# ScalarE's instructions in the written order from batch 2 on, and a wider spacing of the softmax steps

## The chip, the cores and the metric

The kernel runs on one core of one Trainium2 chip. The metric is device time in microseconds for one execution of the whole program. Times without another source are from a profiled execution of the kernel before, counted from the start of its span. TensorE, VectorE, ScalarE and GpSimd compute; SyncE issues the transfers here.

## The reference

There are two parts: an attention over 32 learned slots, and a two-layer network (with ELU between the layers) on its result.

```
a    = softmax(phi, over the 576 positions)          # 8 batches, 8 heads, 576 x 32
k_m  = a^T k ;  v_m = a^T v                          # 32 x 64 per head
attn = softmax(q k_m^T / 8, over the 32 slots)       # 576 x 32
x    = attn v_m                                      # put together: 4608 x 512
h    = x w_in                                        # 4608 x 2048
g    = where(h > 0, h, exp(min(h, 0)) - 1)
out  = g w_out                                       # 4608 x 512
```

All is float32.

## The kernel before, in words

**The work.** The kernel never forms x. For each batch it multiplies `v_m` into `w_in` (the function `vw`), so that `hidden` gets h from the softmax's probabilities (the tile `A`) and that product in one step. A float32 product is made of three matmuls on a high and a low part of each factor, each in the faster format F32R. So nearly every operand is split in two instructions: a cast to the high part on ScalarE (a name with `_high` or `_parts`) and, on VectorE, a subtraction that leaves the low part (`_low`).

**The units.** The output is worked through in units, each half a batch by one block of 128 of the 2,048 hidden channels: 32 units a batch, counted on through the batches by the number `it`. In a half batch, 256 of its 288 rows go through `project2` at once; the 32 that are left over ("rest") are kept in the tile `rest` and multiplied after every second batch by `rest_project`. One unit from batch 2 on is this chain: `hidden` (L711, TensorE, into one of two banks `psh`), `elu_relu` (L835, ScalarE), `elu_exp2` (L840, ScalarE), `elu_max2` (L847 for the 256 rows and L849 for the rest, VectorE). L847 and L849 are the last readers of the bank, so a `hidden` waits for those of two units before. Two units make a pair. For a pair follow four sums on GpSimd (L859 to L862), the casts and remainders of the pair itself (`direct_parts`, L885 and L887, tile `GP` or `gS`) and of the sums (`sum_parts`, L893 and L894, tile `gS`), and on TensorE `project2` (L912), some three units after the pair's `hidden`. In batches 3 to 7, six of eight pairs of a half batch are multiplied in seven products instead of eight, which is what the sums are for.

**The attention of the next batch** is done between the units of the one before: `phi_max` (L441), `phi_exp` (L446), `e_shift` (GpSimd, L323), `e_exp` (ScalarE, L328), `slots` (L487), then for each of three parts of the batch `scores` (L536, into two banks `psb`), `turn` (VectorE, L559, which frees them), the softmax's steps `softmax_max`, `_shift`, `_exp` (ScalarE, L578), `_sum` (L584), `_divide`, `turn_back` (L601), and `probs_high` (ScalarE, L618) and `probs_low` (L626), which write `A`. Four times a batch comes `vw` (L536 too, also into `psb`) with `vw_high` (L656) and `vw_low` (L662). In batch 2, `w_out` is also combined for the seven products: `build_full` and `build_sums` on GpSimd (L789 to L798), `build_high` (L804), `build_low` (L811), and `save_t`, a store that SyncE issues.

**The rest products.** After every second batch come eight times `rest_high` (L1038), `rest_low` (L1043) and `rest_project` (L998), into two turns each of the tiles `GP` and `gS`, then `rest_store` (L1059) and its store. Two `hidden` of the next batch stand among the products on TensorE.

**What sets the order.** Up to the start of batch 2 the order of all engines is a long list, `FIRST`, written out by hand. From there `plan` is a list of steps, each with a place, a number in units:

```
def at(place, f, *a):
    if (f, a) not in done:
        plan.append((place, len(plan), f, a))
...
at(x, hidden, it)
at(x + 0.00001, elu_relu, it)
...
at(it - 0.4 + part, project2, it, part)
```

The plan is sorted by place. TensorE's instructions and SyncE's transfers stand exactly in that order. For ScalarE, VectorE and GpSimd the framework's scheduler chooses the order before the program runs: it takes the earliest step in the plan of those that its own reckoning says could start. At run time each engine takes its instructions in the order that was chosen, and an instruction that waits holds up those behind it.

Of the kernel before, what the change touches and what calls it, by code (L numbers as in the profile page):

```python
# [175 lines left out]
def fused_kernel(ctx: ExitStack, tc: tile.TileContext, phiT, phi, kv0, kvt, kv, q0, q1, w_in, w_out, out):  # L176
# [929 lines left out]
# [4 lines that stand above are left out]
    def softmax(b, u, o, step):  # L1110
        at(o, turn, b, u)
        at(o + step, softmax_max, b, u)
        at(o + 1.01 * step, softmax_shift, b, u)
        at(o + 2 * step, softmax_exp, b, u)
        at(o + 3 * step, softmax_sum, b, u)
        at(o + 3.01 * step, softmax_divide, b, u)
        at(o + 4 * step, turn_back, b, u)
        at(o + 5 * step, probs_high, b, u)
        at(o + 6 * step, probs_low, b, u)
# [6 lines left out]
    def attention(b, o):  # L1126

        x = 1 if b > NB else 0
        at(o - 4, load_phi, b)
        for c in range(NCH):  # L1130
            at(o - 3 + 5.5 * x + (1 - 0.2 * x) * c, load_kv, b, c)
        for u in range(3):
            at(o + 4 + 7.5 * x + u - 0.3 * x * u, load_q, b, u)
            at(o - 3 + u, load_e, b, u)
            at(o + 1.1 + 5.4 * x + u, e_shift, b, u)
            at(o + 2.1 + 5.4 * x + u, e_exp, b, u)
        at(o + 0.1 - 2 * x, phi_max, b)
        for g in range(2):
            at(o + 0.12 - 2 * x, phi_exp, b, g)
        at(o + 1.1, slot_scale, b)  # L1140
        at(o + 1 - 2.4 * x, spread_max, b)
        if b > NB:
            at(o + 2.2, fetch_max, b)
        for c in range(NCH):
            at(o + 5.4 + 5.8 * x, slots, b, c)
        at(o + 6.1 + 5.8 * x, slots_copy, b)
        at(o + 7.2 + 5.8 * x, slots_transpose, b)
        at(o + 7.4 + 5.8 * x, kv_copy, b)
        for u in range(3):
            i = o + 8.2 + 6.7 * x + (2 - 0.2 * x) * u  # L1150
            at(i, scores, b, u)
            softmax(b, u, i + 0.7, 0.3)

    LEAD = 30
    for b in range(2, B):
        base = 2 * NJ * b
        attention(b, 43 if b == 2 else base - LEAD)
        for c in range(NVC):
            for h in range(2 if b > NB else 0):
                at(base - 17 + 4 * c + h, load_w, b, c, h)  # L1160
            products(b, c, base - 10 + 4 * c if b > NB or c < 3 else base - 1.4)
# [58 lines left out]
                at(it + 4.6, rest_out, b // 2)  # L1220

    plan.sort(key=lambda x: x[:2])
    with tc.manual_schedule(engines={mybir.EngineType.PE, mybir.EngineType.SP}):
        with tc.manual_schedule():
            for f, a in first:
                f(*a)
        for _, _, f, a in plan:
            f(*a)
# [43 lines left out]
```

## Time and profile before

| | us |
|---|---|
| median of 3 runs | 769.75 (766.83 to 769.96) |
| the profiled execution | 768.35 |
| its span | 766.6 |
| TensorE busy (matmuls) | 711.2 |
| VectorE busy | 537.3 |
| ScalarE busy | 474.5 |
| GpSimd busy | 205.3 |

The span runs from the first to the last instruction; 1.75 us of the profiled execution lie outside it. Batch 2 begins at about 219 us. A row of a timeline gives start, duration, engine, line, operation, output tile and inputs, shapes and count; in brackets is the time for which the engine had been idle, and what ended it. A row with x12 stands for 12 instructions. A row of a table by stretches gives, after the length, the busy time (and count) of TensorE, its weight loads, VectorE, ScalarE and GpSimd, then the granted clock of TensorE, the share of the DMA engines and GB/s. A row of waits gives who waited for whom, the total in us, how often, and the longest.

### The profile page before, as it was taken

The page shows a single profiled execution, that of the slowest core. Times are in us where ns is not written, and L with a number is a line of the kernel's source. Part 1 is how long each engine was busy: PE and PEld are TensorE (multiplying, and loading weights), DVE is VectorE, ACT ScalarE, POOL GpSimd, SP SyncE. Part 2 cuts the span into 40 slices and gives each one's busy share as a digit, 9 for nine tenths or more (in the row PEclk, how much of TensorE's full clock was granted, in tenths as well). Part 3 has the DMA queues.
Part 4 walks back from the last instruction along what each step waited for, and adds up shares of the span by engine and source line. Part 5 has one row for each costly group of instructions (what it writes and reads, how often), then busy time and mean ns, then how long its engine had stood idle before and what let it go on. Part 6 is the DMA issues. An engine that isn't in the chain of part 4 may idle for free.

```text
span 766.6 us, 15955 instructions
## 1 busy us (share of the span) xinstructions
PE 711.2 (93%) x5974; PEld 604.8 (79%) x5974; DVE 537.3 (70%) x1329; ACT 474.5 (62%) x1146; POOL 205.3 (27%) x364
## 2 busy tenths in 40 slices
PE   7698999999987998999999999989999999999997
PEld 5566787878656876889788887888788988789996
DVE  3999898885674578556875568765786457875653
ACT  3779888886454556665565655665556555566661
POOL 0011111122036631242231432333231242323330
PEclk8799999999998999999999999999999999999999
DMA  9942526153354274786673976678848488464641
GB/s 296 350 175 80 195 81 241 63 204 90 117 127 144 90 275 166 234 310 259 249 278 114 305 276 251 267 233 292 312 173 286 127 298 315 181 242 172 220 165 41
DMA packets 44476, 158.97 MB, mean 207 GB/s; under 512 B 5232, under 2 KB 13552, under 8 KB 35952
## 3 DMA queue, kind: packets, MB, share of 16 engines
q1 hardware_dynamic: 44400, 157.97, 58.4%
q8 instruction: 47, 0.77, 0.4%
q14 instruction: 29, 0.24, 0.1%
HBM read 138.02 MB, written 19.93 MB: 206 GB/s over the span
## 4 chain that ended last, share of the span: by engine, by line
PE 54%; DVE 19%; POOL 9%; ACT 8%; DMA 5%; issue 4%; SPq 1%; DVEq 0%; ACTq 0%; POOLq 0%
PE psh L711 18%; PE pso L912 18%; PE pso L998 13%; DVE G L847 3%; PE psb L536 2%; POOL GF L861 2%; ACT gS L893 2%; PE psb L487 2%; POOL e L323 2%; POOL GF L859 2%; POOL GF L862 2%; DMA raw<-w_out 2%; DVE vw L662 1%; DMA kvt<-kvt 1%; DVE mx L566 1%
## 5 line engine op out<-in xcount | busy, mean ns | idle before, releaser
L711 PE MATMUL psh<-A,vw 128*128 128x288 f32 x1536 | 258.2, 305 | 24.4 <-DVE rest L849 18.5
L711 PEld LDWEIGHTS psh<-A,vw 128*128 128x128 f32 x1536 | 224.2, 191 | 60.7 <-issue 15.8
L912 PE MATMUL pso<-wout,gS 128*128 128x512 f32 (+1 forms) x612 | 145.5, 367 | 0.0
L998 PE MATMUL pso<-wout,GP 128*128 128x512 f32 x504 | 133.6, 400 | 3.2 <-DVE GP L757 2.3
L912 PEld LDWEIGHTS pso<-wout,gS 128*128 128x128 f32 x612 | 104.4, 191 | 14.6 <-ACT GP L885 0.8
L847 DVE SCALAR_TENSOR_TENSOR G<-G,psh 128x256 f32<-128x256 f32 x192 | 79.8, 416 | 48.6 <-ACT G L840 43.9
L998 PEld LDWEIGHTS pso<-wout,GP 128*128 128x128 f32 x504 | 90.1, 188 | 28.3 <-DVE GP L757 3.4
L835 ACT ACTIVATE G<-psh 128x288 f32<-128x288 f32 x192 | 77.6, 405 | 45.2 <-PE psh L711 42.8
L860 POOL TENSOR_TENSOR GF<-G 128x128 f32<-128x128 f32 x60 | 28.7, 479 | 231.3 <-DVE G L847 231.3
L840 ACT ACTIVATE G<-G 128x288 f32<-128x288 f32 x192 | 85.2, 444 | 4.8
L894 DVE TENSOR_TENSOR gS<-GF,gS 128x512 fp32r<-128x512 f32 x60 | 41.6, 693 | 51.8 <-ACT gS L893 51.5
L912 PE MATMUL pso<-tt,gS 128*128 128x256 f32 x540 | 75.8, 282 | 0.0
L893 ACT CAST gS<-GF 128x512 fp32r<-128x512 f32 x60 | 37.2, 621 | 61.4 <-POOL GF L862 59.4
L741 POOL COPY rest<-GF 128x32 f32<-128x32 f32 x64 | 24.4, 382 | 170.8 <-DVE GF L735 170.8
L912 PEld LDWEIGHTS pso<-tt,gS 128*128 128x128 f32 x540 | 69.9, 189 | 0.0
L887 DVE TENSOR_TENSOR GP<-G,GP 128x256 fp32r<-128x256 f32 (+1 forms) x120 | 55.8, 503 | 15.2 <-ACT GP L885 15.2
L912 PE MATMUL pso<-wout,GP 128*128 128x256 f32 x360 | 56.1, 288 | 0.0
L885 ACT CAST GP<-G 128x256 fp32r<-128x256 f32 (+1 forms) x120 | 36.8, 349 | 25.5 <-DVE G L847 20.8
L912 PEld LDWEIGHTS pso<-wout,GP 128*128 128x128 f32 x360 | 50.4, 196 | 0.0
L859 POOL TENSOR_TENSOR GF<-G 128x128 f32<-128x128 f32 x60 | 28.8, 479 | 67.2 <-DVE G L847 54.1
L662 DVE TENSOR_TENSOR vw<-psb,vw 128x512 fp32r<-128x512 f32 (+2 forms) x74 | 42.0, 602 | 2.4 <-ACT vw L656 2.2
L887 DVE TENSOR_TENSOR gS<-G,gS 128x512 fp32r<-128x512 f32 x36 | 26.5, 735 | 21.3 <-ACT gS L885 21.3
(135 smaller groups left out, 999.3 us busy)
## 6 DMA issues: line engine op xcount, KB each, us to landing
tt<-td SPq DMA_DIRECT2D x60, 1024.0 KB, 4.9
wt<-wd SPq DMA_DIRECT2D x40, 512.0 KB, 6.5
kvt<-kv SPq DMA_DIRECT2D x32, 512.0 KB, 8.5
out<-osb SPq DMA_DIRECT2D x16, 512.0 KB, 5.0
raw<-w_in SPq DMA_DIRECT2D x15, 512.0 KB, 7.3
raw<-w_out SPq DMA_DIRECT2D x15, 512.0 KB, 8.0
qt<-q SPq DMA_DIRECT2D x18, 384.0 KB, 5.2
td<-tt SPq DMA_DIRECT2D x6, 1024.0 KB, 4.9
```

Of the source, the lines that this page charges most:

```text
L662: nc.vector.tensor_tensor(t[:, LO, a, n0:n1], ps, t[:, HI, a, n0:n1], ALU.subtract)
L711: nc.tensor.matmul(ps, t[:, x, g, c0 : c0 + P], s["A"][hf][:, y, g, :], start=(n == 0), stop=(n == 5),)
L835: nc.scalar.activation(G[:, it % 2], gs[it], AF.Relu, scale=-1.0)
L840: nc.scalar.activation(G, G, AF.Exp, scale=-1.0)
L847: nc.vector.scalar_tensor_tensor(G[:, :n], G[:, :n], -1.0, ps[:, :n], ALU.add, ALU.max)
L859: eng.tensor_tensor(S[:, 0], a21, a22, ALU.add)
L885: nc.scalar.copy(f(HI), src)
L887: nc.vector.tensor_tensor(f(LO), src, f(HI), ALU.subtract)
L893: nc.scalar.copy(g[:, HI], S)
L894: nc.vector.tensor_tensor(g[:, LO], S, g[:, HI], ALU.subtract)
L912: nc.tensor.matmul(banks[bank_name][:, c0:c1], lhs(y), rhs(x), start=bank_name not in seen_banks, stop=stop and n == 2, skip_group_check=True,
L998: nc.tensor.matmul(ps, gp[:, y], wout[j][:, x, :], start=(first and n == 0), stop=(last and n == 2),)
```

## The change

```
-            softmax(b, u, i + 0.7, 0.3)
+            softmax(b, u, i + 0.7, 0.4)
...
-    with tc.manual_schedule(engines={mybir.EngineType.PE, mybir.EngineType.SP}):
+    with tc.manual_schedule(engines={mybir.EngineType.PE, mybir.EngineType.SP, mybir.EngineType.Activation}):
```

The first line moves the places of the softmax's steps: from `turn` on, they stand 0.4 instead of 0.3 of a unit apart, so `softmax_exp` stands 0.8 after `turn`, `probs_high` 2.0. `turn` itself stays. The second line takes ScalarE's order from the plan, word for word, as TensorE's and SyncE's are. VectorE and GpSimd are still ordered by the scheduler, which now reckons with another ScalarE. TensorE's order is the same instruction for instruction, and no instruction is added or taken away.

On ScalarE at the start of batch 2, from the second unit's Relu on. L1059 is `rest_store`, L804 `build_high`, L885 the first two pairs' `direct_parts`. Before:

```order
L1059 COPY orest<-pso_2511 128x512
L835 ACTIVATE G<-psh 128x288
L840 ACTIVATE G<-G 128x288
L656 CAST vw<-psb 128x512 x3
L804 CAST tt<-FE 128x512
L656 CAST vw<-psb 128x512
L885 CAST gS<-G 128x512
L835 ACTIVATE G<-psh 128x288
L804 CAST tt<-FE 128x512
L840 ACTIVATE G<-G 128x288
```

Now:

```order
L835 ACTIVATE G<-psh 128x288
L840 ACTIVATE G<-G 128x288
L656 CAST vw<-psb 128x512 x4
L835 ACTIVATE G<-psh 128x288
L840 ACTIVATE G<-G 128x288
L835 ACTIVATE G<-psh 128x288
L840 ACTIVATE G<-G 128x288
L1059 COPY orest<-pso_2511 128x512
L885 CAST gS<-G 128x512
```

The four `vw` casts and the next two units' Relu and Exp come first; `build_high` has gone back behind the twelfth unit, and the three `e_exp`, which stood behind the fifth unit, to places between the thirteenth and the sixteenth.

On ScalarE at the end of a softmax (that for batch 4 here; it is alike for batches 5 to 7). L656 is `vw_high`, L618 the last `probs_high`. Before:

```order
L893 CAST gS<-GF 128x512
L835 ACTIVATE G<-psh 128x288
L656 CAST vw<-psb 128x512
L840 ACTIVATE G<-G 128x288
L835 ACTIVATE G<-psh 128x288
L840 ACTIVATE G<-G 128x288
L618 CAST A<-pr 128x2x192
L885 CAST GP<-G 128x256
```

Now:

```order
L893 CAST gS<-GF 128x512
L835 ACTIVATE G<-psh 128x288
L840 ACTIVATE G<-G 128x288
L656 CAST vw<-psb 128x512 x2
L618 CAST A<-pr 128x2x192
L835 ACTIVATE G<-psh 128x288
L840 ACTIVATE G<-G 128x288
```

Relu and Exp of the first unit are no longer parted by a `vw_high`; `probs_high` has moved ahead of Relu and Exp of the second.

On ScalarE at the rest products after batch 3 (after batch 5 it is alike). L1038 is `rest_high`, L1059 `rest_store`; the L885 and L893 are the first pair's of the new batch. Before:

```order
L1038 CAST GP<-rest 128x256
L1038 CAST gS<-rest 128x256
L885 CAST GP<-G 128x256
L893 CAST gS<-GF 128x512
L835 ACTIVATE G<-psh 128x288
L840 ACTIVATE G<-G 128x288
L835 ACTIVATE G<-psh 128x288
L840 ACTIVATE G<-G 128x288
```

These are the seventh and the eighth `rest_high`. Now:

```order
L835 ACTIVATE G<-psh 128x288
L840 ACTIVATE G<-G 128x288
L835 ACTIVATE G<-psh 128x288
L840 ACTIVATE G<-G 128x288
L1038 CAST GP<-rest 128x256
L1038 CAST gS<-rest 128x256
L1059 COPY orest<-pso_4774 128x512
L885 CAST GP<-G 128x256
L885 CAST GP<-G 128x128
L446 ACTIVATE ph,sums<-ph,nm 128x576 x2
L893 CAST gS<-GF 128x512
```

The seventh and eighth `rest_high` now stand behind the two units whose `hidden` stand among the rest products on TensorE, and the first pair's casts behind `rest_store` and, for L893, behind both `phi_exp` (L446).

## The prediction

> **What bounds the kernel now.** I read, in this order, busy time by stage, who waited for whom, and the timelines round each stall of TensorE. First the stages from batch 2 on, summed (190 to 767 us).
>
> ```profile
> sum 577.00, PE 538.06 PEld 466.19 DVE 381.36 ACT 329.83 POOL 177.76; mean PE 89.68 PEld 77.70 DVE 63.56 ACT 54.97 POOL 29.63
> ```
>
> TensorE (second column) is busy for 538.06 of the last 577 us, ScalarE (fifth) for 329.83. So the time is TensorE's work in its fixed order plus its stalls, here 39 us; a new order on ScalarE can change only these, and what it makes other engines late for. Who ends them:
>
> ```profile
> PE psh L711 <- DVE rest L849: 18.5, 17, 5.1
> PE psb L536 <- DVE sc L559: 12.1, 7, 2.6
> ```
>
> `hidden` (L711) waits for VectorE to free one of two `psh` banks, and `scores` or `vw` (L536) for `turn`. VectorE does both only when ScalarE has done Relu and Exp in time. Eighteen microseconds and twelve are all that could be won there. A stall costs a second time:
>
> ```profile
> 374.00:377.40 3.40, 3.29 (x26) 2.67 (x27) 3.19 (x9) 2.21 (x6) 0.00 (x0) 0.58 0.73 290
> ...
> 296.00:299.40 3.40, 3.40 (x12) 2.94 (x12) 3.33 (x10) 3.17 (x8) 0.00 (x0) 0.51 0.46 189
> ...
> 649.00:652.40 3.40, 1.56 (x23) 0.95 (x22) 3.33 (x10) 1.45 (x4) 0.00 (x0) 1.00 1.05 430
> ```
>
> The third figure from the end is the granted clock. After stalls of 1.83 us (at 374) and 2.63 us (at 294) it was about half for 3.4 us, which is 1.7 us of work lost; after one of 1.84 us (at 651) it stayed at 1.00. I price a new stall of 1.8 to 2 us at half of 1.7, and one above 2.5 us at 1.7.
>
> **The change part by part.** No instruction is added or removed; TensorE's, and the loads', orders stay. All costs are shifts. Steady pairs keep ScalarE's order and cost nothing.
>
> *Start of batch 2.*
>
> ```profile
> 226.44 1.86 PE L711 MATMUL psh<-A,vw 128*128 128x288 f32 x12
> 233.43 1.78 PE L711 MATMUL psh<-A,vw 128*128 128x288 f32 x6 [5.12 <-DVE rest L849]
> ...
> 243.36 1.04 PE L711 MATMUL psh<-A,vw 128*128 128x288 f32 x6 [1.03 <-DVE rest L849]
> ...
> 225.98 0.59 ACT L656 CAST vw<-psb 128x512 fp32r<-128x512 f32 x1 [1.42 <-PE psb L536]
> 228.24 0.62 ACT L804 CAST tt<-FE 128x512 fp32r<-128x512 f32 x1 [1.67 <-POOL FE L797]
> 228.76 0.58 ACT L656 CAST vw<-psb 128x512 fp32r<-128x512 f32 x1
> 229.24 0.62 ACT L885 CAST gS<-G 128x512 fp32r<-128x512 f32 x1
> 229.76 0.41 ACT L835 ACTIVATE G<-psh 128x288 f32<-128x288 f32 x1
> ...
> 239.84 0.63 ACT L328 ACTIVATE e<-e 128x512 f32<-128x512 f32 x1 [3.70 <-POOL e L323]
> ...
> 323.69 0.88 PE L912 MATMUL pso<-tt,gS 128*128 128x256 f32 x6
> ```
>
> Before, `build_high` (L804) waits 1.67 us for GpSimd ahead of a Relu whose product was done at 227.4. Now the four `vw` casts end at 227.0, two Relu and Exp (0.85 us a pair) at 228.35 and 229.2, VectorE's two instructions after the first at 228.95, and `hidden` starts at 229.1, not 233.43. The row at 243.36 then falls near 237, since the wait at 239.84 and the half clock go as well: **-6.4**. `build_high` now waits some 10 units later; what covers it is that what it builds (`tt`) is first used in batch 3, at 323.69. If that cover failed, a store of about 5 us would stand in SyncE's queue before the loads of batch 3.
>
> *Softmax done during batch 2.*
>
> ```profile
> 286.51 0.79 PE L536 MATMUL psb<-qt,kvm 64*32 64x192 f32 x16 [1.29 <-DVE sc L559]
> ...
> 294.53 1.33 PE L536 MATMUL psb<-wt,kvm 64*32 64x256 f32 x32 [2.63 <-DVE sc L559]
> ...
> 289.61 1.22 DVE L811 TENSOR_TENSOR tt<-FE,tt 128x512 fp32r<-128x512 f32 x1
> ```
>
> `build_low` (L811) leaves its place ahead of the second and third `turn`. Followed through VectorE's new order with the durations of these rows, they come 1.0 and 3.0 us earlier, and the half clock after 294.53 goes: -4.7. At its end `probs_high` then holds up a Relu, as in the next part: a stall of 1.9 us and 0.85 of clock. Together **-2.0**.
>
> *The four later softmaxes* (batches 4 to 7).
>
> ```profile
> 374.11 1.00 PE L536 MATMUL psb<-qt,kvm 64*32 64x192 f32 x16 [1.83 <-DVE sc L559]
> ...
> 387.19 1.04 PE L711 MATMUL psh<-A,vw 128*128 128x288 f32 x6 [0.87 <-DVE rest L849]
> ...
> 389.14 0.96 PE L711 MATMUL psh<-A,vw 128*128 128x288 f32 x6
> ...
> 385.58 0.41 ACT L835 ACTIVATE G<-psh 128x288 f32<-128x288 f32 x1
> 386.02 0.44 ACT L840 ACTIVATE G<-G 128x288 f32<-128x288 f32 x1
> 387.59 0.52 ACT L618 CAST A<-pr 128x384 fp32r<-128x384 f32 x1 [1.12 <-DVE pr L601]
> ...
> 385.38 0.69 DVE L662 TENSOR_TENSOR vw<-psb,vw 128x512 fp32r<-128x512 f32 x1
> 386.98 0.58 DVE L601 STREAM_TRANSPOSE pr<-sc 128x384 f32<-128x384 f32 x1
> ```
>
> Three shifts. The first Exp of the scores now stands behind a pair's casts, its row sum follows on VectorE, and the second `turn` ends 0.7 us later: the stall of 1.83 becomes 2.5. Next the Exp ahead of the row at 387.19 no longer waits behind a `vw` cast, so that stall of 0.87 goes. Last, `probs_high` (L618) stands ahead of the Relu at 385.58. It waits for L601, which VectorE now does behind both `vw_low` (L662, 0.69 each): it ends about 388.85. So that Relu starts at 389.3, VectorE's L847 at 390.2 and L849 ends at 390.75; the `hidden` of 389.14 starts at 390.8 and the next one is 2.2 us late. From there TensorE runs with everything 2.2 us later. With half of 1.7 for the clock, 3.05 each: **+12.2**.
>
> *The rest products* (after batches 3 and 5).
>
> ```profile
> 413.46 1.77 PE L711 MATMUL psh<-A,vw 128*128 128x288 f32 x12
> 415.07 1.56 PE L998 MATMUL pso<-wout,GP 128*128 128x512 f32 x6
> ...
> 418.66 0.88 PE L912 MATMUL pso<-tt,gS 128*128 128x256 f32 x6
> ...
> 406.11 0.78 ACT L446 ACTIVATE ph<-ph,nm 128x576 f32<-128x576 f32 x1 [1.12 <-DVE nm L441]
> ...
> 410.87 0.41 ACT L1038 CAST gS<-rest 128x256 fp32r<-128x256 f32 x1 [0.99 <-PE pso L998]
> ...
> 413.71 0.62 ACT L893 CAST gS<-GF 128x512 fp32r<-128x512 f32 x1 [1.03 <-PE pso L998]
> ...
> 415.71 0.44 ACT L840 ACTIVATE G<-G 128x288 f32<-128x288 f32 x1
> ...
> 418.07 0.59 ACT L1059 COPY orest<-pso 128x512 f32<-128x512 f32 x1 [0.82 <-PE pso L998]
> ```
>
> Before, all eight `rest_high` (L1038) and the first pair's casts end by 414.3. Now the seventh and eighth `rest_high` stand behind Relu and Exp of the two `hidden` at 413.46, so behind 415.71: the seventh ends at 416.45, its remainder on VectorE, behind two L847 and L849, at 417.1, where TensorE wanted the first at 415.07. That is 1.85 us. Then L1059 waits for the last rest product (1.6 us after its start at 418.3), and the first pair's L885 (0.55), both `phi_exp` (0.77 each from start to start) and only then L893 follow: 419.9 + 0.5 + 0.55 + 1.54 = 422.5, ended at 423.1, its remainder at 423.85. The product of 418.66 cannot pass its first matmul before that: 5.1 us late, of which 3.2 is one stall, so 1.7 for the clock. Two such places: **+13.6**. Queued behind the waiting L893 are the second pair's casts and the next Relu; they keep up again within two pairs.
>
> *Single casts.*
>
> ```profile
> 513.52 1.04 PE L711 MATMUL psh<-A,vw 128*128 128x288 f32 x6 [0.80 <-DVE rest L849]
> ...
> 693.69 1.04 PE L711 MATMUL psh<-A,vw 128*128 128x288 f32 x6 [0.64 <-DVE rest L849]
> ```
>
> At both a Relu stood behind two `vw` casts; now it is ahead, and the stalls of 0.80 and 0.64 go; `phi_exp` and `e_exp` trade places with about nothing between them: **-1.4**.
>
> The sum: -6.4 - 2.0 + 12.2 + 13.6 - 1.4 = +16.0 us. Made against the profiled execution's 768.35 us (span 766.6 and 1.75 outside), it gives 784.4; the median of the runs, 769.75, is 1.4 above that execution. I predict **784 us**.
>
> The Trainium skill, in "TensorE: Matmul & The Clock Gate", section HAM oscillation, asks only that TensorE not idle for more than about 3.4 us. By that, no new stall here would cost clock. The row at 374 disagrees: 1.83 us sufficed. By the rule the sum is the first rival's below; by the row it stays.
>
> **Rivals.**
>
> *The clock holds.* As at 651, none of the new stalls halves the clock. Then 3.4 at the rests, 3.4 at the four softmaxes and 0.85 in batch 2 go: 776.7. For it: that one row. Against it: two stalls of 1.83 and 2.63 that did, and the new ones reach 3.2.
>
> *The softmax comes out even.*
>
> ```profile
> 374.00:381.00 7.00, 6.89 (x65) 6.07 (x73) 6.58 (x19) 3.94 (x10) 0.46 (x1) 0.76 0.36 143
> ```
>
> VectorE (fourth) works 6.58 of 7 us there, so a Relu that waits for L618 may only move work that VectorE would have done late anyway. Without the 12.2: 772.2, near no change. Against it: L847 behind a late Relu is what frees `psh`, and there are two banks.
>
> *Faster, by stock.*
>
> ```profile
> 389.77 0.62 ACT L893 CAST gS<-GF 128x512 fp32r<-128x512 f32 x1 [0.85 <-POOL GF L862]
> ...
> 393.40 0.87 PE L912 MATMUL pso<-wout,GP 128*128 128x256 f32 x6
> ```
>
> If TensorE had converted pairs in hand at the six places, it would run on while ScalarE waits, as between a pair's last cast at 389.77 and the pair's first product at 393.40. Then both positive terms go, the four 0.87 stalls go too, and batch 2's softmax wins its whole 4.7: 768.35 - 6.4 - 4.7 - 3.5 - 1.4 = 752.3. It decides from 3 us of stock. Against it: the products at 415.07 and 418.66 need exactly the casts that are moved, and none is in hand.
>
> *Backlog.* Each late place leaves ScalarE one pair behind; GpSimd's sums then come late for another pair, about 2 us more at six places: 796.
>
> **How the numbers follow.** Forecast 0.60, with its own spread of 778 to 790; clock 0.12; even 0.10; faster 0.07; backlog 0.11. A range of 772 to 794 leaves out the faster case, most of the backlog and a little of the rest. Half a percent, 3.8 us, is about what a measurement tells from no change: faster by more 0.08, within 0.11, slower by more 0.81.
>
> **What would show it.** Right: no stall above 1.5 us between 226 and 245, L811 after 245; TensorE waiting for L1038 or L1043 and then for L893 or L894 after batches 3 and 5; ScalarE waiting for L601 ahead of a Relu once a batch; more half-clock stretches after 300 us. Wrong: `rest_project` starting on time, or the `hidden` after the last `probs_high` within 0.5 us of its bank's turn; then the positive terms fall and the time is below 772.

## The result, and the profile after

The change makes the kernel slower: 790.94 us (median of 4 runs, 789.95 to 796.46) against 768.35 (4 runs, 766.83 to 769.96), a ratio of 1.031 with a 95% interval of 1.025 to 1.036. The forecast was 784 with a range of 772 to 794. The profiled execution took 790.94 us with a span of 789.2 (before: 768.35 and 766.6), at a mean granted clock of 0.970 (before 0.976).

The work is the same, so the 22.6 us between the two spans are waits and clock. From 190 us to the end, in the columns that the prediction's first row has:

```profile
sum 599.30, PE 543.15 PEld 471.04 DVE 387.24 ACT 332.66 POOL 177.83; mean PE 543.15 PEld 471.04 DVE 387.24 ACT 332.66 POOL 177.83
```

TensorE is busy 5.1 us longer than before (543.15 against 538.06), which is lower clock (nine windows of 3.41 us at half clock where there were six, 1.7 us each), and idle for 56 us where it had been idle for 39. Who ends its waits (microseconds in total, times, longest):

```profile
PE psh L711 <- DVE rest L849: 17.3, 12, 2.2
PE psb L536 <- DVE sc L559: 15.8, 8, 3.0
PE pso L912 <- ACT gS L893: 4.8, 2, 2.4
PE psh L711 <- ACT G L835: 4.5, 4, 1.1
...
PE pso L998 <- ACT GP L1038: 2.5, 2, 1.3
...
PE pso L912 <- DMA tt<-td: 2.0, 1, 2.0
```

The first two rows stood in the profile before with 18.5 and 12.1. The other four are new: a rest product waits for a cast (L1038), a pair's products for the cast of their sums (L893), `hidden` for a Relu (L835), and once, for 2.0 us, for a load (before, one such wait took 0.4). The timeline of TensorE shows where they stand; in brackets is the wait ahead of each row.

```profile
228.59 1.03 PE L711 MATMUL psh<-A,vw 128*128 128x288 f32 x6 [0.83 <-DVE rest L849]
...
325.34 0.62 PE L912 MATMUL pso<-tt,GP 128*128 128x256 f32 x3 [1.97 <-DMA tt<-td]
...
347.52 1.03 PE L711 MATMUL psh<-A,vw 128*128 128x288 f32 x6 [1.13 <-ACT G L835]
...
371.69 0.79 PE L536 MATMUL psb<-qt,kvm 64*32 64x192 f32 x16 [2.99 <-DVE sc L559]
...
387.52 1.78 PE L711 MATMUL psh<-A,vw 128*128 128x288 f32 x6 [2.23 <-DVE rest L849]
...
416.15 2.03 PE L998 MATMUL pso<-wout,GP 128*128 128x512 f32 x6 [1.27 <-ACT GP L1038]
...
422.79 0.38 PE L912 MATMUL pso<-tt,gS 128*128 128x256 f32 x1 [2.41 <-ACT gS L893]
```

TensorE's order is the same in both kernels, so any of its instructions can be found in both timelines, and how far it has moved says what lay before it. The table compares such instructions at the borders of the places that the prediction speaks of.

| place | the instruction at its end, before and after | moved there | the term measured | predicted |
|---|---|---|---|---|
| up to 226 us | L711, 226.44 and 225.91 | -0.5 | -0.5 | 0 |
| start of batch 2 | L912, 246.45 and 240.21 | -6.2 | -5.7 | -6.4 |
| softmax in batch 2 | L711, 319.65 and 312.78 | -6.9 | -0.6 | -2.0 |
| start of batch 3 | L912, 345.03 and 340.68 | -4.4 | **+2.5** | 0 |
| `e_exp`, four batches | first L487, 353.19 and 349.56 | -3.6 | **+3.8** (0.7, 1.0, 1.0, 1.0) | 0 |
| four later softmaxes | first L711, 396.87 and 396.61 | -0.3 | +13.4 (3.4, 3.7, 2.8, 3.5) | +12.2 |
| two rest products | first L912, 432.20 and 437.02 | +4.8 | +12.9 (5.1, 7.8) | +13.6 |
| single casts, three places | last L711, 700.06 and 722.49 | +22.4 | -3.1 | -1.4 |

For terms with several places the row names the end of the first (of the last for the single casts). Before rounding they make 22.6. What moved outside these places cancels: +0.8 at a wait of 1.00 us at 508.37 before, which has grown to 1.81 behind two `phi_exp`, and -1.1 between 603 and 622, with small steps elsewhere. The five that the prediction priced come to +16.9 where it had +16.0. What it lacks are the two rows in bold.

### The profile page after: what moved, and what is told of

It is laid out like the page before. It is cut to its first block, busy times and chain, and to the rows that moved or that the text cites. A ratio compares the mean times of both kernels' runs of the same rounds, so it can differ in the third digit from the quotient of the medians.

```text
span 789.2 us, 15976 instructions
## 1 busy us (share of the span) xinstructions
PE 715.6 (91%) x5974; PEld 608.9 (77%) x5974; DVE 543.1 (69%) x1329; ACT 477.7 (61%) x1146; POOL 205.3 (26%) x364
## 4 chain that ended last, share of the span: by engine, by line
PE 48%; DVE 19%; ACT 14%; POOL 8%; DMA 6%; issue 5%; SPq 0%; DVEq 0%; POOLq 0%; ACTq 0%
PE pso L912 16%; PE psh L711 15%; PE pso L998 12%; ACT G L840 3%; DVE G L847 3%; PE psb L536 3%; ACT G L835 3%; ACT gS L893 3%; POOL GF L861 3%; POOL GF L859 2%; POOL GF L862 2%; PE psb L487 2%; DVE vw L662 1%; DMA raw<-w_out 1%; DMA win<-w_in 1%
## 5 line engine op out<-in xcount | busy, mean ns | idle before, releaser
L711 PE MATMUL psh<-A,vw 128*128 128x288 f32 x1536 | 259.3, 305 | 26.8 <-DVE rest L849 17.3
L711 PEld LDWEIGHTS psh<-A,vw 128*128 128x128 f32 x1536 | 225.7, 192 | 60.7 <-ACT G L835 15.8
L912 PE MATMUL pso<-wout,gS 128*128 128x512 f32 (+1 forms) x612 | 144.3, 364 | 1.4 <-DVE gS L887 1.3
L998 PE MATMUL pso<-wout,GP 128*128 128x512 f32 x504 | 134.6, 401 | 6.1 <-ACT GP L1038 2.5
L847 DVE SCALAR_TENSOR_TENSOR G<-G,psh 128x256 f32<-128x256 f32 x192 | 80.4, 419 | 76.6 <-ACT G L840 70.9
L912 PEld LDWEIGHTS pso<-wout,gS 128*128 128x128 f32 x612 | 103.7, 190 | 16.1 <-DVE gS L887 1.6
L998 PEld LDWEIGHTS pso<-wout,GP 128*128 128x128 f32 x504 | 90.0, 188 | 32.8 <-ACT GP L1038 3.9
L835 ACT ACTIVATE G<-psh 128x288 f32<-128x288 f32 x192 | 77.6, 404 | 56.1 <-PE psh L711 55.2
L860 POOL TENSOR_TENSOR GF<-G 128x128 f32<-128x128 f32 x60 | 27.6, 460 | 235.2 <-DVE G L847 228.2
L912 PE MATMUL pso<-tt,gS 128*128 128x256 f32 x540 | 80.9, 294 | 5.3 <-ACT gS L893 4.8
L894 DVE TENSOR_TENSOR gS<-GF,gS 128x512 fp32r<-128x512 f32 x60 | 41.5, 692 | 56.0 <-ACT gS L893 55.8
L912 PEld LDWEIGHTS pso<-tt,gS 128*128 128x128 f32 x540 | 74.5, 200 | 6.3 <-ACT gS L893 5.3
L893 ACT CAST gS<-GF 128x512 fp32r<-128x512 f32 x60 | 37.2, 620 | 69.3 <-POOL GF L862 69.3
L887 DVE TENSOR_TENSOR GP<-G,GP 128x256 fp32r<-128x256 f32 x120 | 56.7, 513 | 21.5 <-ACT GP L885 21.5
L885 ACT CAST GP<-G 128x256 fp32r<-128x256 f32 x120 | 36.4, 350 | 35.4 <-DVE G L847 25.8
L912 PE MATMUL pso<-wout,GP 128*128 128x256 f32 x360 | 55.8, 287 | 0.0
L859 POOL TENSOR_TENSOR GF<-G 128x128 f32<-128x128 f32 x60 | 31.9, 531 | 83.0 <-DVE G L847 83.0
L912 PEld LDWEIGHTS pso<-wout,GP 128*128 128x128 f32 x360 | 50.1, 194 | 0.0
L735 DVE SCALAR_TENSOR_TENSOR GF<-GF,psh 128x288 f32<-128x288 f32 x64 | 28.8, 451 | 16.8 <-ACT GF L729 15.5
```

The lines of the kernel that those rows point to most:

```text
L711: nc.tensor.matmul(ps, t[:, x, g, c0 : c0 + P], s["A"][hf][:, y, g, :], start=(n == 0), stop=(n == 5),)
L835: nc.scalar.activation(G[:, it % 2], gs[it], AF.Relu, scale=-1.0)
L847: nc.vector.scalar_tensor_tensor(G[:, :n], G[:, :n], -1.0, ps[:, :n], ALU.add, ALU.max)
L859: eng.tensor_tensor(S[:, 0], a21, a22, ALU.add)
L885: nc.scalar.copy(f(HI), src)
L887: nc.vector.tensor_tensor(f(LO), src, f(HI), ALU.subtract)
```

## The experiments

All are timed against the kernel before on the same chip, in three rounds; medians of the kernel before lie between 767.4 and 768.2 us. In all of them TensorE's and SyncE's orders are those of the changed kernel. The changed kernel's own runs spread from 789.95 to 796.46 us, so differences of a few us between medians are read together with the shift of TensorE's instructions in the profiled executions. VectorE's order is the scheduler's and moves a little with each edit: in the kernels with one mend 2 to 14 of VectorE's 1,329 instructions stand elsewhere than in the changed kernel, but 89 where both softmax edits are made and 123 with the step at 0.3. What the theory says: every place in ScalarE's written order has a price of its own, and each can be undone by itself. The rivals are in the expectations.

**One half of the change at a time.**

```diff
-            softmax(b, u, i + 0.7, 0.4)
+            softmax(b, u, i + 0.7, 0.3)
```

> The changed kernel with the softmax step back at 0.3: only ScalarE's order is changed. By my theory (each place in ScalarE's order has its own price; the places of the rest products, of e_exp and of the start of batch 3 do not hang on the step, the last probs_high does, since at 0.3 its turn_back stands ahead of both vw_low) 783 us: the changed kernel's 791 less half of the 13.4 us that the four later softmaxes cost there. Rival one, that the step is what costs: near the kernel before, 768 to 771. Rival two, that the step is nothing: 790.

787.65 us, ratio 1.026 (1.023 to 1.029): between the theory's number and rival two's. The other half, the step without ScalarE's order:

```diff
-    with tc.manual_schedule(engines={..., mybir.EngineType.SP, mybir.EngineType.Activation}):
+    with tc.manual_schedule(engines={..., mybir.EngineType.SP}):
```

> The kernel before with the softmax step at 0.4 and ScalarE's order left to the scheduler. By my theory the scheduler puts probs_high and Exp where their inputs come, so the step alone moves little: 768 +- 3 us. Rival one (the step costs): 780 or more.

770.26 us, ratio 1.004 (1.001 to 1.006), as the theory said. So ScalarE's order is nearly all of the change. By the medians the step adds some 3 us on top of it, but the two intervals overlap (1.023 to 1.029, 1.025 to 1.036). By TensorE's instructions the four later softmaxes cost 8.1 us with the step at 0.3 where they cost 13.4. That is 5.3 us less, where I expected half of the term: at 0.3 the wait behind the last `probs_high` shrinks from 2.23 to 1.26, but the first one stays. The timeline of TensorE with ScalarE's order alone, for the softmaxes of batches 4 and 5 and the rest products between them:

```profile
369.95 1.13 PE L536 MATMUL psb<-qt,kvm 64*32 64x192 f32 x16 [2.90 <-DVE sc L559]
...
413.30 2.03 PE L998 MATMUL pso<-wout,GP 128*128 128x512 f32 x6 [1.27 <-ACT GP L1038]
...
419.94 0.39 PE L912 MATMUL pso<-tt,gS 128*128 128x256 f32 x1 [2.41 <-ACT gS L893]
...
490.28 1.04 PE L711 MATMUL psh<-A,vw 128*128 128x288 f32 x6 [1.26 <-DVE rest L849]
```

**The rest products.**

```diff
-                    at(it + 0.61 + 0.01 * i, rest_high, b // 2, i)
-                    at(it + 0.611 + 0.01 * i, rest_low, b // 2, i)
+                    y = it + 0.61 + 0.01 * min(i, 5) + 0.002 * max(i - 5, 0)
+                    at(y, rest_high, b // 2, i)
+                    at(y + 0.001, rest_low, b // 2, i)
...
-                at(it + 0.81, rest_store, b // 2)
+                at(it + 1.35, rest_store, b // 2)
...
+                if b % 2 == 0 and b > NB and hf == 0 and j == 1:
+                    x, y = it - 1.3352, 0.0001
...
-            at(o + 0.12 - 2 * x, phi_exp, b, g)
+            at(o + (3.95 * g - 0.05 if b in (5, 7) else 0.12 - 2 * x), phi_exp, b, g)
```

(`slot_scale`, VectorE's step behind both `phi_exp`, and `sum_parts` move along with them.)

> The changed kernel with the places behind batches 1, 3 and 5 mended on ScalarE: the seventh and eighth rest_high ahead of the two Relu and Exp, the first pair's casts behind them, rest_store behind the second pair's first cast, and the phi_exp of batches 5 and 7 moved into later pairs. By my theory the stalls ahead of L998 (1.27) and L912 (2.41) and the half clock behind them go, 12.9 us in two places: 778 us. Rival (the stalls only move to the next late instruction of VectorE, as TensorE had no stock): 786 or more.

777.11 us, ratio 1.011 (1.008 to 1.014). The timeline of TensorE has no wait left at the place:

```profile
412.62 1.77 PE L711 MATMUL psh<-A,vw 128*128 128x288 f32 x12
414.23 1.56 PE L998 MATMUL pso<-wout,GP 128*128 128x512 f32 x6
415.63 1.56 PE L998 MATMUL pso<-wout,gS 128*128 128x512 f32 x6
417.03 0.96 PE L711 MATMUL psh<-A,vw 128*128 128x288 f32 x6
417.82 0.88 PE L912 MATMUL pso<-tt,gS 128*128 128x256 f32 x6
```

Against the kernel before, both places now cost nothing to within 0.1 us (TensorE's L711 at 396.87 before has moved by -0.74 there, the L912 at 432.20 by -0.84). The term is shown, and the rival with it excluded: the waits did not come back elsewhere.

**The softmaxes.** Once with both edits, once with the last `probs_high` alone.

```diff
-        at(o + 2 * step, softmax_exp, b, u)
+        early = b > NB and u == 0
+        at(o + (0.2 if early else 2 * step), softmax_exp, b, u)
...
-        at(o + 5 * step, probs_high, b, u)
-        at(o + 6 * step, probs_low, b, u)
+        p = o + ((2.35, 2.15, 2.75)[u] if b > NB else 5 * step)
+        at(p, probs_high, b, u)
+        at(p + 0.4, probs_low, b, u)
```

(With `softmax_max` and `softmax_shift` of the first unit likewise at 0.1 and 0.11.)

> The changed kernel with ScalarE's places in the softmaxes of batches 3 to 7 mended: the first Exp of the scores ahead of a pair's casts, and each probs_high behind the Relu that it held up (the last one by 0.75 of a place, between a pair's casts). By my theory the stall of 2.23 us behind the last probs_high and the growth of the first stall from 1.83 to 3.0 go: 11 us of 13.4, so 780 us. Rival (VectorE is full there, so the Relu that waited only moved work that is late anyway): 788 to 791.

```diff
-        at(o + 5 * step, probs_high, b, u)
-        at(o + 6 * step, probs_low, b, u)
+        p = o + (2.75 if b > NB and u == 2 else 5 * step)
+        at(p, probs_high, b, u)
+        at(p + 0.4, probs_low, b, u)
```

> The changed kernel with only the last probs_high and probs_low of the softmaxes of batches 3 to 7 moved, behind the Relu that waited for them. By my theory this alone takes away the stall of 2.23 us behind it in the four later softmaxes and of 1.82 in the first, with some half clocks: 780 us, and the first stall of 3.0 stays. Rival (the first Exp behind a pair's casts makes all of it late): 787 or more.

Both edits: 777.60 us, ratio 1.013 (1.010 to 1.016). `probs_high` alone: 785.34, ratio 1.024 (1.021 to 1.027). The timeline of TensorE in the softmax of batch 4, first with both edits and then with `probs_high` alone:

```profile
369.69 1.13 PE L536 MATMUL psb<-qt,kvm 64*32 64x192 f32 x16 [1.97 <-DVE sc L559]
...
383.71 1.04 PE L711 MATMUL psh<-A,vw 128*128 128x288 f32 x6
...
387.76 1.04 PE L711 MATMUL psh<-A,vw 128*128 128x288 f32 x6 [0.56 <-DVE rest L849]
```

```profile
386.71 1.03 PE L711 MATMUL psh<-A,vw 128*128 128x288 f32 x6 [0.74 <-DVE rest L849]
...
390.75 1.04 PE L711 MATMUL psh<-A,vw 128*128 128x288 f32 x6 [0.57 <-DVE rest L849]
```

With both, the first wait is back to 1.97 (1.83 before the change) and the four softmaxes take as long as before the change. With the second edit alone the wait of 2.23 becomes 0.74 and 0.57, the wait of 2.99 stays, and the gain is 5.6 us of 13.3, not the 11 that I expected of it. So the term has two parts. By the medians the place of the last `probs_high` is worth 5.6 us and the rest of the edits, above all the first Exp behind a pair's casts, 7.7; by TensorE's instructions at the four softmaxes (13.4 us in the change, 6.3 with `probs_high` alone, -0.4 with both) it is 7.1 and 6.7. They are about equal. The second part is not shown to be ScalarE's order alone, since VectorE's order moves with it. The rival "it comes out even" fell.

**The start of batch 2**, put back:

```diff
+        z = 62.61 if n == 0 else x
+        at(z, build_full, p)
+        at(z + 0.02, build_sums, p)
+        y = 63.37 if n == 0 else x + 3.1
+        at(y, build_high, p)
+        at(y + 0.1, build_low, p)
```

> The changed kernel with the first build put back ahead: both build_high casts of pair 0 stand directly behind the vw casts and ahead of the Relu of the first hidden of batch 2, so that ScalarE waits there for GpSimd as in the kernel before. By my theory this takes back the gain at the start of batch 2 (5.7 us by the shift of TensorE's instructions): a stall of 4.5 to 5.5 us near 228 and half clock behind it, 797 us. Rival (the gain came from somewhere else in ScalarE's new order there, as the phi_exp or the casts of the pair): 791 to 793.

795.35 us, ratio 1.036 (1.033 to 1.039), 4.4 us over the changed kernel. ScalarE (first fence) waits for GpSimd ahead of the Relu again, and `hidden` (second) for both:

```profile
230.22 0.62 ACT L804 CAST tt<-FE 128x512 fp32r<-128x512 f32 x1 [1.73 <-POOL FE L798]
230.74 0.40 ACT L835 ACTIVATE G<-psh 128x288 f32<-128x288 f32 x1
```

```profile
232.65 1.78 PE L711 MATMUL psh<-A,vw 128*128 128x288 f32 x6 [4.72 <-DVE rest L849]
```

By TensorE's instructions this gives back 4.6 of 5.7 us. So most of the gain is the place of this first build ahead of a Relu. The edit moves its steps on GpSimd (`build_full`, `build_sums`) and VectorE (`build_low`) too, and the other 1.1 us are open.

**The two unpriced terms.**

```diff
-            at(o + 2.1 + 5.4 * x + u, e_exp, b, u)
+            at(o + 2.1 + 5.4 * x + u + (0.45, 0.01, 0.45)[u] * x, e_exp, b, u)
...
-            at(o + 0.12 - 2 * x, phi_exp, b, g)
+            at(o + (3.95 * g - 0.05 if b in (4, 6) else 0.12 - 2 * x), phi_exp, b, g)
```

(`slot_scale` moves with `phi_exp` here too.)

> The changed kernel with only e_exp (first and third of batches 3 to 7 behind a pair's first casts, the second behind its Relu and Exp) and the phi_exp of batches 4 and 6 moved on ScalarE, out of the way of a Relu. By my theory (an Exp of 0.6 us ahead of a Relu whose product waits holds TensorE up once a batch, and two phi_exp do so after batches 3 and 5's neighbours) the stalls of 1.12 before L711 (ended by L835) and of 1.4 ahead of phi_exp's Relu go: 4 x 0.9 + 3 x 1.4 less what was there before, 784 us. Rival (Relu was late for another reason, the pair's sums on GpSimd): 789 to 791.

```diff
-        at(x + 3.1, build_high, p)
+        y = x + (1.45 if n == 5 else 3.1)
+        at(y, build_high, p)
```

> The changed kernel with the last build_high and build_low 1.65 places earlier. By my theory the wait of 1.97 us for a tt load at the start of batch 3 is the store of the last built tt, which stands in SyncE's queue ahead of the loads of batch 3; 2 us earlier it takes the wait and the half clock behind it (1.7) along: 788 us. Rival (that load was late behind the small transfers of spread_max, whatever the store did): 790 to 791.

The first: 786.31 us, ratio 1.023 (1.019 to 1.027), 4.6 less than the change and 2 short of what I expected. The four waits of 1.13 are gone, and with them all 3.8 us of their term. Of the waits that a Relu behind `phi_exp` made, the one near 518 fell from 1.81 to 0.30. The one near 320 fell from 1.39 to 0.05, but TensorE then met the load behind it earlier and waited there instead (2.24, with one of 0.99 behind it): the start of batch 3 costs 2.2 us where it cost 2.5. The wait of 1.47 near 442, which the kernel before had too (1.30), I had counted among them wrongly. No `phi_exp` stands there; the Relu follows an L893 that waits for GpSimd's sum in both kernels, and the wait is 1.36 now.

The second: 791.35 us, ratio 1.030 (1.026 to 1.033), no change. At the place the wait of 1.97 for the load is gone and one of 0.22 stands at the next load. But the transfer that stands ahead of this load in SyncE's queue (L304, which waits for VectorE's maximum over phi) left almost when it did, at 315.50 where it was 315.79, though the store had landed 1.6 us earlier. The load landed 1.3 us earlier, and TensorE came there 1.2 us later in this execution. What the store contributes to the 2.5 us at the start of batch 3 is open.

**All mends together.** The four edits in one kernel; then the same with `turn` directly behind `scores`; then also with the first `vw` casts of a batch behind the next Relu:

```diff
-        at(o, turn, b, u)
+        at(o - 0.6 if b > NB else o, turn, b, u)
```

```diff
+        z = 1.55 if b > NB and c == 0 and not cols else 0.75
+        at(o + z, vw_high, b, c, *cols)
+        at(o + z + 0.01, vw_low, b, c, *cols)
```

> The changed kernel with all four mends at once (rest products, softmaxes, e_exp and phi_exp, last build). If the prices are separate terms, 791 - 13.8 - 13.3 - 5 - 2 = 757 us, faster than the kernel before (768). Rival (the mends overlap, since each stall hides the next late instruction): 765 or more.

> As the one with all four mends, and the turns of the scores of batches 3 to 7 put directly behind their scores in VectorE's priorities, ahead of the sum, divide and turn_back of the unit before. By my theory the stall of 1.83 to 1.97 us that both kernels have in each softmax comes from VectorE's order and not from ScalarE's: it goes, and half clocks behind it with it, 8 to 13 us: 746 us. Rival (the turn that comes first only makes the row sum and so the Relu's max late): 755 to 760.

> As the one with all four mends and the early turns (750.7 us), and the first vw casts of batches 3 to 7 placed behind the next Relu. By my theory the stall of 0.9 us ahead of the hidden there (four times, ended by Exp L840) goes: 747 us. Rival (vw's bank is then free too late for the next product): 750 to 753.

755.78 us, ratio 0.983 (0.980 to 0.986): the terms add up to within 4 us, as the theory said. Taken singly the mends gained 13.8, 13.3, 4.6 and -0.4 us by the medians, which makes 31.3; together they gain 35.2. The start of batch 3 is one place where they do not simply add: by TensorE's instructions it costs 2.5 us in the change, 2.2 and 0.8 with one of its two mends, and 0.2 with all. The second, 750.68, ratio 0.976 (0.972 to 0.980): half of what was expected, since `turn` (L559) now stands behind a pair's L894, L847 and L849 instead of the whole unit before, and the wait of 1.99 becomes 0.92 and not 0. TensorE's timeline and VectorE's of this kernel:

```profile
365.53 0.79 PE L536 MATMUL psb<-qt,kvm 64*32 64x192 f32 x16 [0.92 <-DVE sc L559]
```

```profile
364.67 0.42 DVE L847 SCALAR_TENSOR_TENSOR G<-G,psh 128x256 f32<-128x256 f32 x1
365.00 0.18 DVE L849 SCALAR_TENSOR_TENSOR rest<-G,psh 128x32 f32<-128x32 f32 x1
365.10 0.64 DVE L559 STREAM_TRANSPOSE sc<-psb 128x192 f32<-128x192 f32 x2
```

And 743.86, ratio 0.969 (0.967 to 0.972), the fastest: 24 us under the kernel before. Its last step is not what I expected it to be. The wait of 0.9 is still there (0.88); it is four waits of 0.56 some 6 us further on that are gone, worth about 1.1 us each. The rest of the 6.8 us is not shown to be the edit's: the two profiled executions part by 3 us in the first 20 us of the program, which it does not touch.

**`turn` alone, in the kernel before**, with the same line:

> The kernel before (step 0.3, ScalarE's order left to the scheduler) with only the turns of batches 3 to 7 placed directly behind their scores. By my theory the stall of 1.83 us in each softmax is VectorE's order in both kernels, so it halves here too and the half clocks at 374, 470 and 555 go with it: 768 - 4 x 0.9 - 5.1 - 2 for batch 2 = 757 us. Rival (without ScalarE's order the Exp comes where it came and the stall stays): 766 to 769.

767.08 us, ratio 1.000 (0.998 to 1.001). This decided nothing. The place of `turn` is only a priority on VectorE, and with ScalarE left to the scheduler no engine's order changed: in the traces every engine takes the same instructions in the same order as in the kernel before (the wait is 1.84, and L559 still follows L601). So these are further executions of the same order, and they show how much chance there is in one: single places of the table differ by up to 0.8 us. That the wait of 1.83 comes from VectorE's order rests on the pair above, where ScalarE's order is written and only `turn` differs; for the kernel before it is argued, not shown.

## Why the prediction was right, and where it was short

The signs that it named all came. Between 226 and 245 us no wait is longer than 1.34, and L811 starts at 248.4; TensorE waits for L1038 and then for L893 at both rest products; ScalarE waits for L601 ahead of a Relu in the softmaxes; and between 300 and 760 us nine windows of 3.41 us have half clock where there were three.

**Start of batch 2**: right. The waits of 5.12 and 1.03 are gone and 0.83 and 1.34 have come, -5.7 for -6.4; the undoing gives most of it back. The wait of 1.34, of a pair's products for L887, was not in the prediction.

**Rest products**: right, nearly to the row. ScalarE's timeline of the changed kernel:

```profile
415.36 0.44 ACT L840 ACTIVATE G<-G 128x288 f32<-128x288 f32 x1
415.71 0.39 ACT L1038 CAST GP<-rest 128x256 fp32r<-128x256 f32 x1
...
419.62 0.59 ACT L1059 COPY orest<-pso 128x512 f32<-128x512 f32 x1 [3.21 <-PE pso L998]
420.10 0.60 ACT L885 CAST GP<-G 128x256 fp32r<-128x256 f32 x2
420.61 0.78 ACT L446 ACTIVATE ph<-ph,nm 128x576 f32<-128x576 f32 x1
...
421.38 0.76 ACT L446 ACTIVATE ph<-ph,nm 128x576 f32<-128x576 f32 x1
...
422.13 0.60 ACT L893 CAST gS<-GF 128x512 fp32r<-128x512 f32 x1
```

I had the seventh `rest_high` end at 416.45 (416.10 here, with everything 0.3 earlier), L893 at 423.1 (422.73), and a delay of 5.1 us: the L912 at 432.20 before has moved by 5.08 against the start of the place. The wait ahead of L998 was 1.27, not 1.85. The clock was put at 1.7 us for each place; the first lost none, and the second, with the same waits, took 2.7 us longer at half clock.

**Four later softmaxes**: right in sum (13.4 for 12.2) and in the mechanism at the last `probs_high`. It held the Relu up, and TensorE waited 2.23 us where I had the `hidden` 2.2 late (three times; in batch 6 the wait is 1.13):

```profile
385.52 0.51 ACT L618 CAST A<-pr 128x384 fp32r<-128x384 f32 x1 [2.16 <-DVE pr L601]
385.94 0.40 ACT L835 ACTIVATE G<-psh 128x288 f32<-128x288 f32 x1
```

The step "the stall of 1.83 becomes 2.5" was too small. It became 2.99. Its cause is as predicted. ScalarE before (first fence) has the first Exp of the scores (L578) ahead of a pair's casts; now (second) the Exp follows L893, which waits for GpSimd:

```profile
368.75 0.52 ACT L578 ACTIVATE sc<-sc 128x384 f32<-128x384 f32 x1 [1.55 <-DVE sc L574]
```

```profile
367.46 0.62 ACT L893 CAST gS<-GF 128x512 fp32r<-128x512 f32 x1 [1.15 <-POOL GF L862]
367.98 0.52 ACT L578 ACTIVATE sc<-sc 128x384 f32<-128x384 f32 x1
```

TensorE stands 3.6 us earlier there than before, so against it the Exp comes 2.8 us later.

**Softmax in batch 2**: half right. The wait of 2.63 fell to 1.18 and one of 1.82 came at the last `probs_high`, as said; but the first of the two `turn`, which I had 1.0 us earlier, was not (1.29 before, 1.38 now). -0.6 for -2.0.

**Single casts**: -3.1 for -1.4. The two priced places gave 1.5. At a third, which I left out, casts and `e_exp` stood ahead of a Relu and between it and its Exp; they no longer do, and the wait of 1.01 at 518.87 before is gone.

**What failed** is a sentence of the single casts: "`phi_exp` and `e_exp` trade places with about nothing between them". In the written order `e_exp` stands ahead of a Relu (second fence); before (first), the Relu followed L893 there:

```profile
349.04 0.62 ACT L893 CAST gS<-GF 128x512 fp32r<-128x512 f32 x1 [1.15 <-POOL GF L862]
349.56 0.41 ACT L835 ACTIVATE G<-psh 128x288 f32<-128x288 f32 x1
```

```profile
344.90 0.62 ACT L893 CAST gS<-GF 128x512 fp32r<-128x512 f32 x1 [1.15 <-POOL GF L862]
345.42 0.63 ACT L328 ACTIVATE e<-e 128x512 f32<-128x512 f32 x1
345.96 0.39 ACT L835 ACTIVATE G<-psh 128x288 f32<-128x288 f32 x1
```

That makes this Relu 0.54 us late, and three of them in three units leave TensorE waiting once a batch: 3.8 us over four batches, shown by the kernel without it. L893 waits 1.15 us for GpSimd's sum in both kernels, so the sums are not the cause. The other missing term is at the start of batch 3. There `phi_exp` (of batch 4) was not priced, since I priced it only where it follows rest products; at 320 it stands ahead of a Relu as well (a wait of 1.39), and behind it TensorE, some 7 us early, met a load that was not there yet (1.97). The prediction named a late load as what would happen if the cover of `build_high` failed and gave it no price. Whether it was the store of `build_high` that was late is not shown. Nor is the size of this term sharp: in the profiled executions of the five other kernels that leave these places of ScalarE's order alone (one with the step at 0.3) it is 1.2 to 2.9 us.

The rivals: *softmax even*, *faster by stock* and *the clock holds* did not occur. *Backlog* (796) is not far off in its number, but the time that was missing lies at `e_exp` and at the start of batch 3, not at pairs behind the six places that it named.

## What to carry to other kernels

In an order written out by hand, every instruction that stands ahead of one that frees a buffer can have a price, be it half a microsecond long. Go through all of them, not only through those whose input is late. Fix such an order before judging it: here four mends of places turned a loss of 3% into a gain of nearly 2%, and their single gains added up to within 4 us. At one place, the start of batch 3, a stall did hide another: with the first gone, TensorE met the second.

## What the runs showed of the clock

I priced a stall by its length: half of 1.7 us at 1.8 to 2 us, all of it from 2.5 up. The runs show another rule. The stretches at half clock begin, in each execution, on a fixed grid of 3.41 us. In the rows of the changed kernel (start and end of a window of that grid, its length, TensorE's busy time; third from the end the granted clock):

```profile
322.58:325.99 3.41, 1.45 (x12) 1.24 (x11) 2.15 (x6) 2.23 (x7) 1.23 (x3) 1.00 1.02 413
325.99:329.40 3.41, 3.41 (x17) 3.41 (x16) 1.73 (x4) 1.23 (x3) 0.00 (x0) 0.50 0.92 375
366.95:370.36 3.41, 1.75 (x15) 1.55 (x13) 2.22 (x8) 2.52 (x6) 0.46 (x1) 1.00 1.02 407
370.36:373.77 3.41, 2.08 (x26) 1.67 (x27) 3.38 (x10) 1.17 (x3) 0.00 (x0) 1.00 0.81 294
...
418.16:421.57 3.41, 2.22 (x13) 1.71 (x11) 0.62 (x2) 1.95 (x6) 0.00 (x0) 1.00 0.00 0
421.57:424.98 3.41, 1.85 (x13) 1.65 (x14) 2.54 (x8) 2.94 (x8) 0.00 (x0) 1.00 0.00 0
612.71:616.12 3.41, 1.08 (x8) 0.80 (x6) 0.96 (x4) 3.09 (x9) 0.00 (x0) 1.00 0.00 0
616.12:619.53 3.41, 3.18 (x13) 2.89 (x14) 2.33 (x6) 1.81 (x6) 0.46 (x1) 0.50 0.00 0
```

In the first window TensorE idles for 1.96 us (3.41 - 1.45), and the next one has half clock. The wait of 2.99 us, the longest, is cut by the border at 370.36 into 1.66 and 1.33, and costs no clock. The two rest products have the same waits (1.27 and 2.41): at 418 the longer one falls into two windows with 1.19 and 1.56 of idle time, at 612 nearly all of it into one with 2.33, and only there the clock halves. Over the profiles of the 14 kernels of this study, from 226 us on, 54 windows at full clock had at least 1.86 us of idle time and 53 of them were followed by half clock; 12 of 18 between 1.75 and 1.86; 5 of 2,055 below that. Where the grid falls changes from execution to execution (the first half clock behind 226 us starts at 231.21 in the kernel before and at 226.59 in the one with the same orders, 4.62 us apart and so not on one grid), so the cost of one stall is a matter of chance, and what counts over many is how many windows come near 1.8 us. In the kernel with all mends there are three such stretches after 226 us, in the two with the early `turn` one and none, where the change has seven (9 windows) and the kernel before five (6 windows). The Trainium skill, in "TensorE: Matmul & The Clock Gate", section What's actually happening, describes such a free-running window of about 3.4 us. Its section HAM oscillation gives as the rule that TensorE should have no idle gap above about 3.4 us. These rows show that this is not enough: the clock halved behind 1.96 and 2.33 us of idle time in one window.
